# Attention's order written anew: products of one array tiling next to each other, memory products over the whole array, the first pair's loads ahead of the constants

## The chip, the cores and the metric

The kernel runs on one core of a Trainium2 chip. The metric is the device time of one execution in microseconds (us). It is one launch; the host only lays out the inputs. TensorE (PE) does matrix products and transposes, VectorE (DVE), ScalarE (ACT) and GpSimd (POOL) work element by element, and SyncE (SP) issues the DMA transfers between HBM and the on-chip memory. Each engine runs its own instructions strictly in order and waits for the others by semaphores.

## The reference

The reference is a chain of three layers in float32. For 4 batches of 8 heads, with 576 tokens and 64 columns a head:

```python
scores = where(causal, -1e9, q @ k.T / 8); a = softmax(scores); local = a @ v
q_p = phi(q)                      # x + 1 where x > 0, else exp(x)
mem_out = (q_p @ M_prev) / (q_p @ z_prev + 1e-6)
x = sigmoid(beta) * mem_out + (1 - sigmoid(beta)) * local      # 2304 tokens x 512
d = softmax over tokens of x @ phi; slots = d.T @ x            # 32 slots
y = softmax over slots of x @ phi  @  per-expert relu(slots @ w1) @ w2
out = (s * relu(y @ w_in)**2 + b) @ w_out
```

The change lies in the first layer, and in how its work meets what runs beside it.

## The kernel before, in words

Attention goes by pairs of heads: 16 pairs, 4 of a batch. A pair's two heads share a tile, one head in rows 0 to 63 and the other in rows 64 to 127. The work of a pair is cut into small parts, and the list `STEP` (L64) is the order in which one pass of the loop at L611 writes them out: `name:k` means that pass `i` does this part for pair `i + k`. So one pass holds parts of up to five pairs, and since PE, ACT, DVE and POOL keep the written order, `STEP` sets what stands behind what on each engine. SP's transfers are placed by the tile framework when their buffers come free.

The parts, with the engine of each:

- `K`, `R` (SP, L248, L255): loads of a pair's keys, and of its queries, values and memory. `LG` (SP, L559): a piece of `w_in` as 64-bit words; at the last pair it also starts 12 loads of expert weights. `LW` (SP): one buffer of expert weights.
- `S0` to `S4` (PE, L282): scores of 128 queries (64 in `S4`) against all earlier keys, for both heads. For `S0` to `S3` the two heads' products use 64 rows by 128 columns of the array each and run side by side; `S4` uses four quarters of 64 by 64. `Dt.h` (DVE, L296) adds the mask, finds the row's maximum and takes the scores out of PSUM; `Et.h` (ACT) makes the exponential and its sum.
- `Tt.h` (PE, L331): transposes of the probabilities over the whole 128 by 128 array, `t + 1` blocks of 128 columns each (`T4.0` three blocks, `T4.1` two). `Ut.h` takes them out of PSUM, on ACT, for `t = 4` on DVE. `scl` (DVE), `pscl` (POOL) scale the last 64 queries' probabilities ahead of `T4`.
- `V` (PE, L383): probabilities times values, in two column halves of 128 by 64; `O0`, `O1` (ACT) take them out.
- `F0`, `F1`, `F2` (POOL, ACT, DVE): the feature map phi(q). `Z` (POOL, L350): two small copies that put the norm vector behind each head's memory. `M` (PE, L357): the memory products, ten of 65 columns, each on 64 rows by 128 columns. `N` (DVE, L367): the division, into the buffer `mo`.
- `C` (PE): five transposes of the local result. `A`, `A4` (DVE), `P` (POOL, in the last pair DVE): scaling and sum. `X` (PE, L425): transposes of the result, four of 128 by 128 and one of 64 by 64. `Y`, `Y2` (DVE, ACT) take them out; `L` (PE, L439): the routing products, four column quarters of 128 by 32; `B` (DVE).
- `W0`, `Wa` to `Wd` (ACT, POOL, DVE): conversion of a piece of `w_in`. Names in small letters (`dx`, `de`, `dT`, `ds`, `du`, ...) run once a batch.

PSUM has two tiles of two banks for `S` and `M` together, three banks for the transposes, `X`, `C`, `L` and part of `V`, and one for the rest of `V`. A part that takes such a tile waits until the tile taken two (or three) parts earlier has been emptied.

After attention come the merge of the routing sums, the experts (L641 to L712) and the feed-forward layer (L714 to L822). The change does not touch them.

Of the kernel before, what the change touches and what calls it, by code (L numbers as in the profile page):

```python
# [17 lines left out]
B, H, S, D = 4, 8, 576, 64  # L18
NPAIR = B * H // 2
# [16 lines left out]
M_MZ = M_V + 640  # L36
M_END = M_MZ + 130
# [24 lines left out]


STEP = """  # L64
U3.0:1 D2.1:2 E0.0:2 S4:2 U0.1:2 F2:1 D4.0:2 X:0 Z:1 Y:0 T4.1:1 E2.0:2 Y2:0 S3:2 U4.1:1 LG:1 W0:1
D4.1:2 L:0 B:0 dx:0 T2.0:2 E1.0:2 T0.0:2 S0:3 D3.0:2 D0.0:3 V:1 E2.1:2 E4.0:2 fac:1 U2.0:2 D3.1:2
de:0 dT:0 U0.0:2 E3.0:2 dU:0 O0:1 Wa:1 Wb:1 scl:2 O1:1 M:1 Wc:1 D0.1:3 R:4 pscl:2 T1.0:2 gT:0 E1.1:2
ds:0 LW:1 Wd:1 N:1 du:0 K:4 U1.0:2 S1:3 gU:0 T4.0:2 C:1 S2:3 U4.0:2 E3.1:2 F0:2 F1:2 A:1 T1.1:2
E0.1:3 P:1 U1.1:2 T2.1:2 A4:1 U2.1:2 D1.0:3 T3.1:2 D1.1:3 T3.0:2 T0.1:3 U3.1:2 D2.0:3
""".split()  # L70

def strided(ap, *dims):

    return bass.AP(ap.tensor, ap.offset, [list(ap.ap[0])] + [list(d) for d in dims])
# [3 lines left out]
def tile_attention_moe_ffn(  # L78
# [16 lines left out]
    PE, ACT, DVE, POOL, SP = nc.tensor, nc.scalar, nc.vector, nc.gpsimd, nc.sync  # L95
# [6 lines left out]
    ident = cs[:, C_ID:C_ID + 128]  # L102
# [88 lines left out]
    last_pe = [None]  # L191
# [39 lines left out]
    OT, mo, xT = MA[:, 0:640], MA[:, 640:1280].rearrange("p (t d) -> p t d", t=5), MA[:, 0:S]  # L231
# [14 lines left out]
    k_t, qvm_t, x_t, st_t, y_t, o_t, u_t, s_t, t_t, m_t = {}, {}, {}, {}, {}, {}, {}, {}, {}, {}  # L246

    def load_keys(p):  # L248
        if p < NPAIR:
            k_t[p] = KA[:, S * (p % 2):S * (p % 2) + S]  # L250
            for h in range(2):
                r = slice(64 * h, 64 * h + 64)
                SP.dma_start(out=k_t[p][r, :], in_=qk[2 * p + h, r, S:2 * S])

    def load_rest(p):  # L255
        if p < NPAIR:
            qvm_t[p] = QA[p % 3]
            SP.dma_start(out=qvm_t[p], in_=qvm[p])

    def pool_copy(dst, src):  # L260
        POOL.tensor_scalar(out=dst, in0=src, scalar1=1.0, scalar2=0.0, op0=ALU.mult, op1=ALU.add)  # L261
# [14 lines left out]
    def stats(p):  # L276

        if p not in st_t:
            st_t[p] = ap2.tile([128, 28], F32, tag="st", name="st", bufs=5)
        return st_t[p]  # L280
# [66 lines left out]
            evac(strided(PT[p % 2][:, 0, 1344 * i + 512:1344 * i + 513], (64 if i else 448, n), (1984, 2), (1, 64)),  # L347
                 strided(tp[:, 0:1], (128, n), (64, 2), (1, 64)), "v")

    def norm_columns(p):  # L350

        mz = qvm_t[p][:, M_MZ:M_END]
        for h in range(2):
            r = slice(64 * h, 64 * h + 64)
            POOL.tensor_copy(mz[r, 64 + 64 * h:65 + 64 * h], mz[r, 128 + h:129 + h])

    def memory(p):  # L357

        f, mz = FI[p % 2], qvm_t[p][:, M_MZ:M_END]
        y = y_t[p] = pS.tile([128, 1024], F32, tag="s", name="s")  # L360
        for t in range(5):
            for h in range(2):
                r = slice(64 * h, 64 * h + 64)
                PE.matmul(y[:, 512 * h + 65 * t:512 * h + 65 * t + 65], f[r, t * 128:(t + 1) * 128], mz[r, 64 * h:64 * h + 65],  # L364
                          start=True, stop=True)

    def memory_out(p):  # L367
        st, ic, y = stats(p), icst[:, p % 4, :], y_t.pop(p)
        c = slice(8, 18)
        DVE.scalar_tensor_tensor(  # L370
            out=st[:, c].rearrange("p (t h) -> p t h", h=2), in0=strided(y[:, 64:65], (65, 5), (512, 2)), scalar=1e-6,
            in1=ic[:, c].rearrange("p (t h) -> p t h", h=2), op0=ALU.add, op1=ALU.mult)
        DVE.reciprocal(out=st[:, c], in_=st[:, c])
        DVE.tensor_tensor(
            out=mo.rearrange("p t (h d) -> p t h d", h=2), in0=strided(y[:, 0:1], (65, 5), (512, 2), (1, 64)),
            in1=strided(st[:, 8:9], (2, 5), (1, 2), (0, 64)), op=ALU.mult)

    def factors(p):
# [46 lines left out]
    def x_transposes(p):  # L425
        x = x_t[p]
        tp, t2 = t_t[p, "y"] = [pT.tile([128, 512], F32, tag="t", name="t") for _ in range(2)]
        for t in range(4):
            PE.transpose(tp[:, t * 128:(t + 1) * 128], x[:, t, :], ident)  # L429
        last_pe[0] = PE.transpose(t2[:, 0:64], x[0:64, 4, :], ident[0:64, 0:64])  # L430

    def x_out(p, part):
        tp, t2 = t_t[p, "y"]
# [105 lines left out]
    def load_next(place_of=None):  # L539

        n, tag = place_of or next(places, (0, None))
        if n and wnext[0] < len(wkeys):
            load_place(n, tag)
            held.append((wnext[0], n, tag))
# [14 lines left out]
    def load_first(p):  # L559
# [3 lines left out]
    tiles = {"S": scores, "D": maxima, "E": exponentials, "T": transposes, "U": transposed}  # L563
    parts = {
        "K": (load_keys,), "R": (load_rest,), "LW": (lambda p: load_next(),), "LG": (load_first,), "scl": (scale_last,),
        "pscl": (scaled_last,), "F0": (feature, 0), "F1": (feature, 1), "F2": (feature, 2), "Z": (norm_columns,),
        "M": (memory,), "N": (memory_out,), "V": (values,), "O0": (values_out, 0), "O1": (values_out, 1),
        "fac": (factors,), "C": (combine,), "A": (added, 0), "A4": (added, 1), "P": (add_memory,),
        "X": (x_transposes,), "Y": (x_out, 0), "Y2": (x_out, 1), "L": (logits,), "B": (logits_out,),
        "W0": (first_weights, 0), "Wa": (first_weights, 1), "Wb": (first_weights, 2), "Wc": (first_weights, 3), "Wd": (first_weights, 4)}  # L570
    batch = {
# [4 lines left out]
    def part_of(name, p):  # L576
# [11 lines left out]
        if p == NPAIR - 1 and name == "LG":  # L588
            for _ in range(12):
                load_next()  # L590

    SP.dma_start(out=cs, in_=cst)
    SP.dma_start(out=bet, in_=beta)
    SP.dma_start(out=phs, in_=phi)
# [28 lines left out]
    def ps_h():  # L623
        return pH.tile([128, 512], F32, tag="h", name="h")
# [4 lines left out]
    t = ps_h()  # L629
# [57 lines left out]
    for b in range(B):  # L687
# [14 lines left out]
            out=csk[:, :, 1:4:2, :], in0=strided(cex[:, 0, 0:1], (NSLOT, 5), (0, 2), (1, NSLOT)),  # L702
            in1=strided(chi[:, 0, 0:1], (NSLOT, 5), (0, 2), (1, NSLOT)), op=ALU.subtract)
        t = ps_h()
# [3 lines left out]
        t = ps_h()  # L708
# [31 lines left out]
    for _ in range(W_BUFS):  # L740
        t = wp.tile([128, 2 * UNIT], F32R, tag="w", name="w")
# [144 lines left out]
```

## Time and profile before

| what | value |
|---|---|
| median of 3 runs | 555.32 us (553.84 to 561.74) |
| profiled execution | 555.2 us, its span 553.4 us |
| busy share of the span | PE 94%, DVE 66%, ACT 51%, POOL 31% |
| chain that ended last | PE 84%, POOL 7%, DVE 4%, issue 2% |
| attention with its merge | 0 to 250 us of the span |
| experts | 250 to 306 us |
| feed-forward layer | 306 to 553 us |

The chain that ended last is the sequence of work, followed back from the last instruction, in which each step waited for the one before it. PE's busy share counts modelled ends of pipelined products, so a busy PE may still be waiting inside between two products; the start times of successive products tell more. The profiled execution is read against its own time of 555.2 us.

### The profile page before, as it was taken

Reading aid. Unit: us, or ns where it says so; the run is one execution under the profiler, and the core shown is the slowest. Engines: PE = TensorE matmul, PEld = TensorE weight load, DVE = VectorE, ACT = ScalarE, POOL = GpSimd, SP = SyncE. Lnnn points to the kernel's source line nnn. Section 1 sums busy time; section 2 is a strip of 40 time slices with the busy share of each in tenths; the row PEclk is TensorE's granted clock in tenths of the full one; section 3 lists DMA queues with packets and bytes.
Section 4 is the critical chain, followed back from the end, with each engine's and each line's share of the span. In section 5 each row is a group of like instructions: output and inputs, shape, how many; then the busy total and the mean of one; then the engine's idle time right before and its main releaser. Section 6 shows DMA issues by size and latency. Waiting matters only on the chain.

```text
span 553.4 us, 9319 instructions
## 1 busy us (share of the span) xinstructions
PE 520.3 (94%) x3255; PEld 345.3 (62%) x3255; DVE 365.5 (66%) x917; ACT 280.4 (51%) x743; POOL 172.3 (31%) x212
## 2 busy tenths in 40 slices
PE   3999999999999999989999788879999999999997
PEld 1466665666566656653332456558888888888885
DVE  2788887888788878750430999983367465473770
ACT  2877777777777767510221765453542422423322
POOL 0233331332233333300000469996430411404103
PEclk9999999999999999997999999898999999999999
DMA  8799342424242413789995342400020010100101
GB/s 263 249 334 343 126 148 72 150 72 149 69 152 72 149 50 115 245 300 381 368 358 181 126 153 76 152 1 1 1 114 1 10 48 0 59 0 1 57 1 57
DMA packets 26622, 72.01 MB, mean 130 GB/s; under 512 B 3024, under 2 KB 3152, under 8 KB 26576
## 3 DMA queue, kind: packets, MB, share of 16 engines
q1 hardware_dynamic: 26576, 71.42, 37.2%
q8 instruction: 26, 0.43, 0.3%
q14 instruction: 20, 0.16, 0.1%
HBM read 66.69 MB, written 4.72 MB: 129 GB/s over the span
## 4 chain that ended last, share of the span: by engine, by line
PE 84%; POOL 7%; DVE 4%; issue 2%; DMA 1%; ACT 1%; SPq 0%; POOLq 0%; DVEq 0%; ACTq 0%
PE y L799 10%; PE y L801 10%; PE y L800 10%; PE s L290 9%; PE t L335 8%; PE o L394 7%; PE s L364 4%; PE y L662 3%; PE s L294 3%; PE y L646 3%; POOL P L781 3%; PE h L770 3%; POOL R L264 2%; PE t L338 2%; PE t L429 2%
## 5 line engine op out<-in xcount | busy, mean ns | idle before, releaser
L801 PE MATMUL y<-w,R 128*128 128x512 f32 x288 | 114.2, 397 | 6.0 <-POOL R L264 6.0
L799 PE MATMUL y<-w,R 128*128 128x512 f32 x288 | 115.7, 402 | 3.9 <-POOL R L261 3.6
L800 PE MATMUL y<-w,R 128*128 128x512 f32 x288 | 114.1, 396 | 1.4 <-DVE w L759 1.4
L774 ACT ACTIVATE P<-h 128x384 f32<-128x384 f32 x96 | 47.1, 492 | 123.9 <-PE h L770 123.9
L781 POOL TENSOR_SCALAR P<-P,sbt 128x384 f32<-128x384 f32 x31 | 34.7, 1120 | 194.6 <-ACT P L776 194.6
L785 DVE SCALAR_TENSOR_TENSOR P<-P,sbt 128x384 f32<-128x384 f32 x58 | 45.0, 776 | 58.6 <-ACT P L774 58.4
L316 ACT ACTIVATE P<-P,st 128x256 f32<-128x256 f32 (+3 forms) x128 | 71.0, 556 | 5.8 <-DVE st L302 5.8
L801 PEld LDWEIGHTS y<-w,R 128*128 128x128 f32 x288 | 54.6, 190 | 23.3 <-POOL R L264 9.8
L799 PEld LDWEIGHTS y<-w,R 128*128 128x128 f32 x288 | 54.7, 190 | 18.9 <-POOL R L261 6.7
L302 DVE CUSTOM_DVE_ANT_0 P<-s,cs 128x128 f32<-128x128 f32 (+3 forms) x128 | 58.7, 480 | 10.5 <-PE s L290 6.1
L800 PEld LDWEIGHTS y<-w,R 128*128 128x128 f32 x288 | 54.9, 191 | 10.9 <-DVE w L759 1.7
L335 PE MATMUL t<-cs,P 128*128 128x128 f32 x320 | 46.1, 282 | 0.8 <-DVE raw L204 0.6
L290 PE MATMUL s<-R,Q 64*128 64x256 f32 (+3 forms) x176 | 36.8, 499 | 9.5 <-DMA R<-in_qk_dram 8.8
L264 POOL TENSOR_TENSOR R<-P,R 128x384 fp32r<-128x384 f32 x38 | 43.2, 1138 | 3.2
L335 PEld LDWEIGHTS t<-cs,P 128*128 128x128 f32 x320 | 34.2, 141 | 14.4 <-DVE x L417 8.0
L787 DVE SCALAR_TENSOR_TENSOR R<-P,sbt,R 128x384 fp32r<-128x384 f32 x58 | 36.9, 636 | 5.8 <-DVE R L786 0.5
L329 POOL TENSOR_SCALAR P<-P,st 128x576 f32<-128x576 f32 x16 | 16.2, 1014 | 67.1 <-DVE st L325 51.5
L770 PE MATMUL h<-x,R 128*128 128x384 f32 x96 | 34.4, 358 | 0.6 <-ACT P L774 0.6
L202 ACT ACTIVATE raw<-t 128x128 f32<-128x128 f32 (+2 forms) x64 | 25.5, 432 | 15.4 <-PE t L335 15.4
L423 POOL TENSOR_TENSOR x<-x,M 128x512 f32<-128x512 f32 x15 | 19.2, 1280 | 44.4 <-DVE x L417 44.4
L202 ACT ACTIVATE PT<-t 128x128 f32<-128x128 f32 (+2 forms) x64 | 25.2, 433 | 10.4 <-PE t L335 10.4
L786 DVE TENSOR_SCALAR R<-P,sbt 128x384 fp32r<-128x384 f32 x58 | 26.4, 455 | 5.9
(232 smaller groups left out, 868.9 us busy)
## 6 DMA issues: line engine op xcount, KB each, us to landing
w<-in_w_dram SPq DMA_DIRECT2D x18, 512.0 KB, 7.1
raw<-in_w_in_dram SPq DMA_DIRECT2D x8, 1024.0 KB, 5.4
w<-in_w_dram SPq DMA_DIRECT2D x32, 256.0 KB, 5.4
Q<-in_qvm_dram SPq DMA_DIRECT2D x11, 673.0 KB, 5.6
R<-in_qk_dram SPq DMA_DIRECT2D x32, 144.0 KB, 2.8
out_dram<-P SPq DMA_DIRECT2D x18, 256.0 KB, 2.0
raw<-in_w_out_dram SPq DMA_DIRECT2D x4, 1024.0 KB, 4.8
R<-in_qvm_dram SPq DMA_DIRECT2D x5, 673.0 KB, 6.5
```

The lines of the kernel that those rows point to most:

```text
L202: ACT.activation(out=dst, in_=src, func=AF.Copy)
L264: POOL.tensor_tensor(out=dst, in0=a, in1=b, op=ALU.subtract)
L290: PE.matmul(ps[:, 512 * h:512 * h + n], q[r, t * 128:(t + 1) * 128], k[r, 0:n], start=True, stop=True)
L302: DVE.tensor_tensor_reduce(out=Pt[h, t], in0=x, in1=cs[:, C_M2 - n:C_M2], scale=-0.125, scalar=BIG, op0=ALU.add, op1=ALU.min, accum_out=st ...
L316: ACT.activation(out=pt, in_=pt, func=AF.Exp, scale=-1.0, bias=st[:, 18 + c:19 + c], accum_out=st[:, c:c + 1])
L335: PE.transpose(tp[:, kb * 128:(kb + 1) * 128], Pt[i, t][:, kb * 128:(kb + 1) * 128], ident)
L770: PE.matmul(hp[:, 0:TG], G(k * 128, 128), cT[:, g * TG:(g + 1) * TG], start=True, stop=True)
L774: ACT.activation(out=r, in_=hp[:, 0:TG], func=AF.Relu)
L781: POOL.tensor_scalar(out=r, in0=r, scalar1=sbt[:, 0:1], scalar2=sbt[:, 1:2], op0=ALU.mult, op1=ALU.add)
L799: PE.matmul(acc[g, i], hi[:, c], who[k], start=(k == 0), stop=False)
L800: PE.matmul(acc[g, i], hi[:, c], wlo[k], start=False, stop=False)
L801: PE.matmul(acc[g, i], lo[:, c], who[k], start=False, stop=(k == NK - 1))
```

## The change

Four things change.

1. `STEP` is a new list. On PE one pass now runs, in this order: `T4.0:1 T3.1:1 T3.0:1 | S4:2 | T0.0:2 X:0 T1.1:2 | S3:2 S0:3 | L:0 | V:1 | T2.0:2 T1.0:2 dT | S1:3 S2:3 | T2.1:2 gT ds C:1 M:2 T0.1:3 T4.1:2`. Before it ran `S4:2 | X:0 T4.1:1 | S3:2 | L:0 | T2.0:2 T0.0:2 | S0:3 | V:1 | dT M:1 | T1.0:2 gT ds | S1:3 | T4.0:2 C:1 | S2:3 | T1.1:2 T2.1:2 T3.1:2 T3.0:2 T0.1:3`. Bars stand where the tiling of the array changes. `M`, the feature map, `LG` and the conversions of `w_in` come one pass earlier for a given pair; `P`, `LW`, `T3`, `T4.0` and what follows from these come later (`LW` by two passes).
2. `M` becomes five products of 130 columns over the whole array, both heads' memories and norms in one (the zeros of the other head are already in the loaded tile). `Z` goes. `N` reads the new places.
3. `X`'s fifth transpose covers 128 by 128 where it covered 64 by 64.
4. Pair 0's keys and its `qvm` tile (in two transfers, the queries first) are loaded ahead of the four constants.

```diff
 STEP = """
-U3.0:1 D2.1:2 E0.0:2 S4:2 U0.1:2 F2:1 D4.0:2 X:0 Z:1 Y:0 T4.1:1 E2.0:2 Y2:0 S3:2 U4.1:1 LG:1 W0:1
-D4.1:2 L:0 B:0 dx:0 T2.0:2 E1.0:2 T0.0:2 S0:3 D3.0:2 D0.0:3 V:1 E2.1:2 E4.0:2 fac:1 U2.0:2 D3.1:2
-de:0 dT:0 U0.0:2 E3.0:2 dU:0 O0:1 Wa:1 Wb:1 scl:2 O1:1 M:1 Wc:1 D0.1:3 R:4 pscl:2 T1.0:2 gT:0 E1.1:2
-ds:0 LW:1 Wd:1 N:1 du:0 K:4 U1.0:2 S1:3 gU:0 T4.0:2 C:1 S2:3 U4.0:2 E3.1:2 F0:2 F1:2 A:1 T1.1:2
-E0.1:3 P:1 U1.1:2 T2.1:2 A4:1 U2.1:2 D1.0:3 T3.1:2 D1.1:3 T3.0:2 T0.1:3 U3.1:2 D2.0:3
+D2.0:2 T4.0:1 T3.1:1 E0.0:2 U4.1:1 E1.1:2 T3.0:1 D2.1:2 U3.1:1 U4.0:1 S4:2 U3.0:1 T0.0:2 LG:2 P:0
+N:1 D4.0:2 E1.0:2 X:0 D4.1:2 Y:0 U0.0:2 T1.1:2 S3:2 Y2:0 E2.0:2 S0:3 fac:1 L:0 U1.1:2 F2:2 V:1 W0:2
+Wa:2 T2.0:2 B:0 E2.1:2 D3.1:2 R:4 F0:3 LW:-1 E4.0:2 E3.1:2 dx:0 D3.0:2 T1.0:2 D0.0:3 de:0 O0:1 Wb:2
+O1:1 D0.1:3 K:4 dT:0 U2.0:2 S1:3 S2:3 U1.0:2 Wc:2 T2.1:2 dU:0 D1.1:3 E0.1:3 gT:0 D1.0:3 ds:0 gU:0
+scl:2 U2.1:2 Wd:2 du:0 F1:3 pscl:2 C:1 A:1 E3.0:2 M:2 T0.1:3 T4.1:2 A4:1 U0.1:3
 """.split()
...
-            for h in range(2):
-                r = slice(64 * h, 64 * h + 64)
-                PE.matmul(y[:, 512 * h + 65 * t:512 * h + 65 * t + 65], f[r, t * 128:(t + 1) * 128], mz[r, 64 * h:64 * h + 65],
-                          start=True, stop=True)
+            PE.matmul(y[:, 191 * t:191 * t + 130], f[:, t * 128:(t + 1) * 128], mz, start=True, stop=True)
...
-        last_pe[0] = PE.transpose(t2[:, 0:64], x[0:64, 4, :], ident[0:64, 0:64])
+        last_pe[0] = PE.transpose(t2[:, 0:128], x[:, 4, :], ident)
...
+            for c in (slice(0, S), slice(S, M_END)) if p == 0 else (slice(0, M_END),):
+                SP.dma_start(out=qvm_t[p][:, c], in_=qvm[p, :, c])
...
+    load_keys(0)
+    load_rest(0)
     SP.dma_start(out=cs, in_=cst)
```

## Rows read from the trace of the kernel before

**Rows 1.** Windows: length, busy PE, PEld, DVE, ACT, POOL; clock, DMA share, GB/s.

```profile
121.22:134.68 13.46, 13.46 (x114) 8.43 (x113) 11.38 (x39) 10.10 (x32) 4.22 (x6) 1.00 0.45 152
250.00:306.00 56.00, 53.33 (x343) 17.20 (x343) 13.64 (x46) 11.41 (x28) 0.00 (x0) 0.95 0.89 324
```

**Rows 2.** Timeline of PE in one pass: start, us to the last end, engine, line.

```profile
121.22 0.49 PE L290 MATMUL s<-R,Q 64*128 64x128 f32 x4
...
124.50 1.33 PE L364 MATMUL s<-Q,R 64*128 64x65 f32 x20
125.76 0.44 PE L335 MATMUL t<-cs,P 128*128 128x128 f32 x2
126.13 0.70 PE L290 MATMUL s<-R,Q 64*128 64x256 f32 x4
126.77 0.55 PE L338 MATMUL t<-cs,P 128*128 128x128 f32 x3
...
127.79 0.92 PE L290 MATMUL s<-R,Q 64*128 64x384 f32 x4
128.64 1.75 PE L335 MATMUL t<-cs,P 128*128 128x128 f32 x14
130.31 1.19 PE L294 MATMUL s<-R,Q 64*64 64x288 f32 x8
131.43 0.66 PE L429 MATMUL t<-cs,x 128*128 128x128 f32 x4
...
132.59 1.13 PE L290 MATMUL s<-R,Q 64*128 64x512 f32 x4
133.65 0.42 PE L442 MATMUL t<-M,phs 128*32 128x128 f32 x8
...
134.68 0.49 PE L290 MATMUL s<-R,Q 64*128 64x128 f32 x4
```

**Rows 3.** Timeline of PE behind the last pair's values.

```profile
233.56 0.88 PE L196 MATMUL s<-cs 128*128 128x64 f32 x6
234.37 1.33 PE L364 MATMUL s<-Q,R 64*128 64x65 f32 x20
235.63 0.66 PE L406 MATMUL t<-cs,M 128*128 128x128 f32 x4
```

**Rows 4.** Groups by line and shape: busy us, mean ns of one, idle before.

```profile
L189 DVE SCALAR_TENSOR_TENSOR win<-raw,win 128x512 int32<-128x512 int32 x16 | 16.2, 1010 | 0.1
...
L417 DVE TENSOR_TENSOR x<-t,st 128x512 f32<-128x512 f32 x16 | 10.9, 681 | 0.0
...
L415 DVE TENSOR_TENSOR x<-t,M 128x128 f32<-128x128 f32 x16 | 4.5, 281 | 0.0
...
L204 DVE COPY PT<-t 128x256 f32<-128x256 f32 x8 | 3.3, 416 | 0.0
...
L324 DVE TENSOR_SCALAR st<-st,eb 128x1 f32<-128x1 f32 x16 | 3.3, 207 | 0.0
```

**Rows 5.** Timeline of DVE, the first pair's maxima.

```profile
9.81 0.29 DVE L302 CUSTOM_DVE_ANT_0 P<-s,cs 128x128 f32<-128x128 f32 x1 [4.31 <-PE s L290]
...
10.66 0.42 DVE L302 CUSTOM_DVE_ANT_0 P<-s,cs 128x256 f32<-128x256 f32 x1 [0.34 <-PE s L290]
11.01 0.08 DVE L302 DVE_READ_ACCUMULATOR2_ANT st<- 128x1 f32 x1
...
12.07 0.56 DVE L302 CUSTOM_DVE_ANT_0 P<-s,cs 128x384 f32<-128x384 f32 x1 [0.63 <-PE s L290]
```

**Rows 6.** Page, DMA issues: count, KB each, median us to landing.

```profile
Q<-in_qvm_dram SPq DMA_DIRECT2D x11, 673.0 KB, 5.6
R<-in_qk_dram SPq DMA_DIRECT2D x32, 144.0 KB, 2.8
...
cs<-in_cst_dram SPq DMA_DIRECT2D x1, 528.0 KB, 3.4
```

**Rows 7.** Timeline of DVE, the last pair's scaling.

```profile
236.95 0.68 DVE L417 TENSOR_TENSOR x<-t,st 128x512 f32<-128x512 f32 x1
```

More of the change, by code (lines that the diff above doesn't have):

```diff
@@ L248, in load_keys @@
     def load_keys(p):
-        if p < NPAIR:
+        if p not in k_t:
             k_t[p] = KA[:, S * (p % 2):S * (p % 2) + S]
@@ L255, in load_rest @@
     def load_rest(p):
-        if p < NPAIR:
+        if p not in qvm_t:
             qvm_t[p] = QA[p % 3]
-            SP.dma_start(out=qvm_t[p], in_=qvm[p])
+            for c in (slice(0, S), slice(S, M_END)) if p == 0 else (slice(0, M_END),):
+                SP.dma_start(out=qvm_t[p][:, c], in_=qvm[p, :, c])
     def pool_copy(dst, src):
@@ L348, in transposed @@
                  strided(tp[:, 0:1], (128, n), (64, 2), (1, 64)), "v")
-    def norm_columns(p):
-        mz = qvm_t[p][:, M_MZ:M_END]
-        for h in range(2):
-            r = slice(64 * h, 64 * h + 64)
-            POOL.tensor_copy(mz[r, 64 + 64 * h:65 + 64 * h], mz[r, 128 + h:129 + h])
     def memory(p):
@@ L361, in memory @@
         for t in range(5):
-            for h in range(2):
-                r = slice(64 * h, 64 * h + 64)
-                PE.matmul(y[:, 512 * h + 65 * t:512 * h + 65 * t + 65], f[r, t * 128:(t + 1) * 128], mz[r, 64 * h:64 * h + 65],
-                          start=True, stop=True)
+            PE.matmul(y[:, 191 * t:191 * t + 130], f[:, t * 128:(t + 1) * 128], mz, start=True, stop=True)
     def memory_out(p):
@@ L370, in memory_out @@
         DVE.scalar_tensor_tensor(
-            out=st[:, c].rearrange("p (t h) -> p t h", h=2), in0=strided(y[:, 64:65], (65, 5), (512, 2)), scalar=1e-6,
+            out=st[:, c].rearrange("p (t h) -> p t h", h=2), in0=strided(y[:, 128:129], (191, 5), (1, 2)), scalar=1e-6,
             in1=ic[:, c].rearrange("p (t h) -> p t h", h=2), op0=ALU.add, op1=ALU.mult)
@@ L374, in memory_out @@
         DVE.tensor_tensor(
-            out=mo.rearrange("p t (h d) -> p t h d", h=2), in0=strided(y[:, 0:1], (65, 5), (512, 2), (1, 64)),
+            out=mo.rearrange("p t (h d) -> p t h d", h=2), in0=strided(y[:, 0:1], (191, 5), (64, 2), (1, 64)),
             in1=strided(st[:, 8:9], (2, 5), (1, 2), (0, 64)), op=ALU.mult)
@@ L565, in tile_attention_moe_ffn @@
         "K": (load_keys,), "R": (load_rest,), "LW": (lambda p: load_next(),), "LG": (load_first,), "scl": (scale_last,),
-        "pscl": (scaled_last,), "F0": (feature, 0), "F1": (feature, 1), "F2": (feature, 2), "Z": (norm_columns,),
+        "pscl": (scaled_last,), "F0": (feature, 0), "F1": (feature, 1), "F2": (feature, 2),
         "M": (memory,), "N": (memory_out,), "V": (values,), "O0": (values_out, 0), "O1": (values_out, 1),
```

## The prediction

> **What bounds the kernel now.** I read the page's chain first: most of it is PE. Then the windows: in a steady attention pass of 13.46 us PE is busy for all of it at full clock (1.00), while DVE has 11.38 us of work, ACT 10.10 and POOL 4.22 [rows 1]. So a pass ends when PE's own list ends, and the question is what PE spends its list on. The timeline of PE answers that, read by start times, since the durations overlap [rows 2].
>
> The score groups start 0.64 us (S1, 126.13 to 126.77), 0.85 (S2) and 1.06 (S3, 132.59 to 133.65) ahead of the group behind them: 0.21 for each further 128 columns, and 0.21 left over that no column explains. Two transposes behind other work take 0.37 (125.76 to 126.13), fourteen take 1.67 (128.64 to 130.31): 0.108 a block and 0.15 left over. The group T4.0 with C behind it (126.77 to 127.79, eight blocks) takes 1.02, which is 8 x 0.108 + 0.15: two different parts with the same tiling pay the rest once. So PE pays about 0.15 us (0.21 where scores stand alone) each time the array's tiling changes, part in running dry, part in loading the first weights with nothing beside it. The other groups, less their columns at the same rate: S4 1.12 - 0.97 = 0.15; S0 and V together (121.22 to 124.50) 3.28 - 0.21 - 2.67 = 0.40; M 1.26, of which ten steps of 0.112 are products, 0.14 left; X with T4.1 behind it (131.43 to 132.59) 1.16 - 7 x 0.108 = 0.40, for three groups, as X's fifth block has a tiling of its own; L about 0.12.
>
> **The change, part by part.** *Fewer changes of tiling.* The old pass has 15 groups: S0 to S3 at 0.21, six of transposes at 0.15, X's fifth block 0.09, S4 0.15, V 0.19, M 0.14, L 0.12, 2.4 us in all. The new one has eight: S4 0.15, three of the whole array at 0.15, S3 with S0 and S1 with S2 at 0.21 each, L 0.12, V 0.19, sum 1.33. PE alone saves 1.1 us, and its pass is 12.35. No trace shows two score groups in a row: bounds for the two seams 0 and 0.21 each; I take 0, as T4.0 with C paid nothing.
>
> *M over the whole array.* Ten steps as before, now 130 columns at 0.21 per two steps of 128, so 0.108 each, against weight loads that already set 0.112. Six plain whole-array products of 64 columns take 0.81 to the next group [rows 3], less 0.15 for the change 0.11 each: the same step. So M keeps 1.12. Between transposes and plain products of one tiling no row shows the seam: bounds 0 and 0.15 for each of two; I take 0.05 together, near the seam that cost nothing.
>
> *Waits.* The new pass has a tight ring. S4 needs the PSUM tile of S2, which D2.1 empties, and DVE's list from S1 on reads D1.1, D1.0, scl, Wd, A, A4, D2.0, U4.1, D2.1. Durations: 2 x 0.42 and 2 x 0.55 [rows 5], about 0.2 and 0.2 for scl's two, 1.01, 0.68, 0.28, 0.42 [rows 4], together 4.7; one starts some 0.08 before the last ends (10.66 to 11.01 for 0.42, [rows 5]), so 4.0 to 4.7. From S1's result to S4, PE has S2 0.74, 22 blocks x 0.108, M 1.12 and 0.15 for the change, less 0.2 us until the result is out: 4.2. PE therefore waits 0 to 0.5 us a pass; I take 0.15, between them. T4.0, T4.1 and T3.0 need PSUM that A, A4 and U4.1 empty in the same stretch, the same wait and not a second one. L needs Y, which now stands behind N on DVE: Y's end and L's turn fall within 0.1 us of each other. A pass is then 12.55, 0.9 less. DVE with 11.4 of 12.55 still has 1.1 us of idle time, ahead of D1.1, where it takes up what is late in the first half.
>
> *Moves that cost nothing while that holds.* The feature map, the conversions of w_in and M go one pass earlier, with the same instructions. LG's 1 MB is issued once Wd has freed its buffer, 5 us ahead of W0, and W0's result isn't wanted for 2 us more. P goes behind A, at the pass's start on POOL, 1.3 us that N's last step and X wait for: A ends 1.5 us before S4, X starts 1.3 after. T4 waits for pscl (1 us on POOL behind scl), with about 0.3 to spare. Z was 0.4 us of idle POOL. R waits for V now, 3 us ahead of need as before. LW's twelve loads go two passes later, on an SP queue with DMA at 0.45 [rows 1]; the last four, and the first tagged places, are issued at the last pair's LG, a pass before they were. The 64-row transposes made 128-row cost the step they had, 0.108.
>
> *Start.* The first maximum runs at 9.81, behind scores that waited for the keys [rows 5]. Ahead of them went constants (528 KB) and qvm (673 KB), then keys of 2 x 144 KB [rows 6]. Now 0.58 MB of about 1.5 MB are enough for S0, but the mask still comes last of the same bytes. So S0 goes 3 to 4 us earlier, the maximum by 8.2 to 8.5 us, 1.4 earlier. With W0 of pair 0 a pass earlier, behind 1 MB, some of ACT's time may be lost again; bounds 0 and 3.5, I take 1.5, near the mask's arrival.
>
> *End.* Between the last pair's V and C stood M, 1.26 us from 234.37 to 235.63 [rows 3], and the division ahead of A (236.95, [rows 7]), which C's result could have fed at about 236.2. Both are now done a pass before. C then follows V's evacuation: 1.3 earlier, and A 0.7 more. I take 2.0; 0 if C's evacuation binds elsewhere, 4 if the gaps ahead of it close too.
>
> **Sum.** 16 pairs, of which the first and last passes are ramps: 14 x 0.9 = 12.6, plus 1.5, plus 2.0, is 16.1. From the profiled 555.2 us (span 553.4; the median of the runs shown is 555.3, so it stands for them) that gives 539. Experts and feed-forward move as a block. In 250 to 306 PE is busy for 53.3 of 56 us with DMA at 0.89 [rows 1], so weights are close to binding there; their buffers come free relative to attention's end, and w_in's and the feature map's a pass earlier, so I add nothing.
>
> **Rivals.** *DVE's ring closes late.* If the ring takes its 4.7 us and one seam costs something, a pass is 13.1 or so: 0.6 more in 14 passes, 547. For it: DVE would be busy for 90% of such a pass, with every wait in order. Against it: its idle time sits ahead of D1.1. Chance 0.17.
>
> *The order saves nothing.* If PE's left-over time goes with each new tile, not with the tiling, only start and end gain: 552. T4.0 with C speaks against it. Chance 0.06.
>
> *The memory products double.* If a product of 130 columns over the whole array can't overlap its weights, M takes 20 steps' time: 1.12 more a pass, 15.7 in all, 555, no change. The six plain products speak against it, with 64 columns only [rows 3]. The Trainium skill (TensorEngine Tiling (Array Packing), Overview) promises up to twice the speed for a contraction of 64 rows cut into two row tiles, which is what the change gives up; by that, M alone would cost this much more. Here weight loads, not columns, set the old step, so no such gain stood in the trace. Chance 0.05.
>
> *The clock falls: slower.* The new pass runs transposes and M together for some 3.7 us (T2.1 to T3.0), where the longest run was 1.67. If PE fell to half its clock in that stretch, it would take 3.7 more in each pass, 51 in 14: 590. It passes the old time from the fifth pass on that falls (16.1 / 3.7). For it: the clock is below 1 around the experts [rows 1]. Against it: 1.00 with fourteen transposes in a row, and M parts the new run. The Trainium skill (TensorE: Matmul & The Clock Gate, Part 4: PE-mode transpose) says that transposes don't count as busy time for the clock in the way products do, which speaks for it; no row here bears it out. Chance 0.05.
>
> **How the numbers follow.** My forecast, PE bound at about 12.5 us a pass, has 0.67: 539, of itself 533 (seams and ring 0: 15.4, start 2.5, end 4) to 544 (the ring's wait at 0.4: 9.1, start and end 1 each). Before and after can be told apart from no change by about 2%, 11 us. The range takes in the ring's case and ends short of the doubled product: 533 to 551, some 8 in 10. Faster by over 2% means under 544: nearly all of 0.67 and a little of the ring's, 0.68. Within 2%: the ring, the order that saves nothing, the doubled product, 0.27. Slower by over 2%: the clock, 0.05.
>
> **What would show it.** Successive S4 starts on PE 12.4 to 12.7 apart in passes without a batch's end, S0 0.22 to 0.23 long behind S3, and steps of 0.11 in M. Waits of PE's S4 or T3.0 for DVE (D2, U4) of 0.1 to 0.2 each would be the ring; over 0.5 make the ring's case. S0 of the first pair near 5 us, its first maximum near 8.4. C of the last pair less than 1 us behind V. The stretch of the experts as long as before, 56 us. The forecast is wrong if the clock's row falls under 1.0 in a pass, if W0 waits for its transfer by more than 2 us, or if the weights arrive late behind a shorter end of attention.

## The result, and the profile after

The changed kernel takes **536.34 us** (median of 4 runs, 534.34 to 538.49) against 558.53 (median of 4, 553.84 to 562.1) in the same comparison: the ratio is 0.9608, 95% interval 0.9505 to 0.9712. It is faster, and the time is 2.7 us under the forecast of 539.0. Run again later in five rounds it gave 538.18 us, ratio 0.9645 (0.9589 to 0.9701). In all comparisons of this study the kernel before took 552.36 to 556.13 us at a mean granted clock of 0.986 to 0.994 and 559.46 to 562.31 us at one of 0.972 to 0.977, so the median of a few of its runs moves with how many of each there are. The profiled executions differ by less than the medians of this comparison: span 553.39 before, 532.55 after (534.34 us with what lies around it), at mean clocks of 0.987 and 0.990. Those 20.8 us are what is taken apart here.

Windows of the kernel after, columns as in [rows 1]: a pass of attention from one S4 to the next, the experts' first layer, and a stretch at half clock.

```profile
163.26:175.70 12.44, 12.44 (x104) 8.52 (x103) 10.79 (x39) 10.21 (x32) 3.57 (x4) 1.00 0.41 143
233.40:248.40 15.00, 15.00 (x133) 4.91 (x136) 0.62 (x1) 1.67 (x3) 0.00 (x0) 1.00 1.04 388
...
289.50:296.30 6.80, 6.49 (x17) 2.96 (x10) 4.85 (x8) 2.33 (x4) 2.79 (x3) 0.50 0.43 154
```

The pass of 13.46 us [rows 1] is now 12.44 (12.44 or 12.45 in each pass without a batch's end, from the third on), still with PE busy for all of it and at full clock. PE of that pass, the rows that answer to [rows 2]; what counts is again the distance from one start to the next.

```profile
163.26 1.19 PE L295 MATMUL s<-R,Q 64*64 64x288 f32 x8
164.37 0.33 PE L336 MATMUL t<-cs,P 128*128 128x128 f32 x1
...
165.44 1.35 PE L291 MATMUL s<-R,Q 64*128 64x512 f32 x8
166.72 0.43 PE L433 MATMUL t<-M,phs 128*32 128x128 f32 x8
...
167.33 2.76 PE L385 MATMUL o<-raw,R 128*64 128x512 f32 x20
...
170.72 1.35 PE L291 MATMUL s<-R,Q 64*128 64x256 f32 x8
171.99 0.55 PE L336 MATMUL t<-cs,P 128*128 128x128 f32 x3
...
172.81 0.27 PE L398 MATMUL t<-cs,M 128*128 128x128 f32 x1
172.92 1.28 PE L356 MATMUL s<-Q,F 128*128 128x130 f32 x10
174.04 0.27 PE L336 MATMUL t<-cs,P 128*128 128x128 f32 x1
...
175.70 0.70 PE L295 MATMUL s<-R,Q 64*64 64x288 f32 x3
```

There are eight groups. S3 with S0 takes 1.28 (165.44 to 166.72): the 1.06 of S3 alone and one step of 0.21 for S0's 128 columns, so the seam between two score groups is nothing. M takes 1.12 from its first product to the next transpose (172.92 to 174.04), and 0.11 separates C's last block from it, the step of a block: no seam on either side.

The end of attention, PE from the last pair's values on (it answers to [rows 3]):

```profile
216.59 2.76 PE L385 MATMUL o<-raw,Q 128*64 128x512 f32 x20
219.28 0.88 PE L196 MATMUL s<-cs 128*128 128x64 f32 x6
220.11 0.66 PE L397 MATMUL t<-cs,M 128*128 128x128 f32 x4
```

The products that keep PE warm run behind the values now and C follows them; M is gone from here. DVE of the same stretch, the scaling of [rows 7]:

```profile
220.80 0.69 DVE L408 TENSOR_TENSOR x<-t,st 128x512 f32<-128x512 f32 x1 [3.86 <-PE t L397]
```

And the start, which answers to [rows 5] and [rows 6]: PE's first scores, DVE's first maximum, then ACT's first piece of w_in (W0), each with what it waited for.

```profile
5.24 1.65 PE L291 MATMUL s<-R,Q 64*128 64x128 f32 x8 [5.24 <-DMA Q<-in_qvm_dram]
...
8.84 0.29 DVE L303 CUSTOM_DVE_ANT_0 P<-s,cs 128x128 f32<-128x128 f32 x1 [8.84 <-DMA cs<-in_cst_dram]
...
15.09 0.69 ACT L181 ACTIVATE win<-raw 128x512 f32<-128x512 f32 x1 [0.26 <-DMA raw<-in_w_in_dram]
```

From the second pair's S2 on PE runs without a gap to the first pair's values. First the kernel before, then after:

```profile
18.75 0.92 PE L290 MATMUL s<-R,Q 64*128 64x384 f32 x4
...
24.99 2.32 PE L394 MATMUL o<-PT,Q 128*64 128x512 f32 x12
```

```profile
17.64 0.92 PE L291 MATMUL s<-R,Q 64*128 64x384 f32 x4 [0.53 <-DVE st L303]
...
18.94 1.38 PE L356 MATMUL s<-Q,F 128*128 128x130 f32 x10
20.16 0.27 PE L336 MATMUL t<-cs,P 128*128 128x128 f32 x1
...
25.14 2.05 PE L385 MATMUL o<-PT,Q 128*64 128x512 f32 x10
```

S2 stands 1.11 us earlier than before, and the values 0.15 later: M of the first pair, 1.22 from 18.94 to 20.16, now comes ahead of them. From S2 to the values it is 6.24 before and 7.50 after; of the runs below, the one in the old order has the same 6.24, and six in the new one 7.49 or 7.50.

**Where the 20.8 us came from**, by the start of the same PE groups in both profiles:

| stretch | before | after | gain |
|---|---|---|---|
| start to pair 0's first values | 24.99 | 25.14 | -0.15 |
| 14 passes, to pair 14's values | 195.91 | 181.94 | 13.97 |
| to the products of the selection (L624) | 27.35 | 24.82 | 2.53 |
| these, to the experts' first layer | 2.19 | 1.50 | 0.69 |
| experts' first layer | 17.38 | 15.01 | 2.37 |
| to the feed-forward's first product | 38.82 | 38.82 | 0.00 |
| feed-forward to PE's last product | 242.31 | 241.28 | 1.03 |
| behind it | 4.44 | 4.04 | 0.40 |

The starts on which the attention rows rest, before (L394, L631) and after (L385, L624); the others stand above:

```profile
220.90 2.79 PE L394 MATMUL o<-PT,R 128*64 128x512 f32 x20
...
230.87 2.76 PE L394 MATMUL o<-raw,Q 128*64 128x512 f32 x20
...
248.25 1.74 PE L631 MATMUL h<-sel,uacc 128*128 128x32 f32 x8 [1.23 <-DVE sel L520]
```

```profile
207.08 2.76 PE L385 MATMUL o<-PT,R 128*64 128x512 f32 x20
...
231.90 1.05 PE L624 MATMUL h<-sel,uacc 128*128 128x32 f32 x8 [1.22 <-DVE sel L511]
```

The -0.15 of the first row is less than what one start differs from another: with the start of the changed kernel the first values came at 25.14, 25.25 and 26.30 in three profiles, with that of before at 24.99 and 26.34 in two. Attention itself gave 16.35 us. The 3.06 about the experts' first layer is the clock, not the order. Two windows of the kernel before show it, the first in that layer's beginning and the second behind it:

```profile
250.44:255.20 4.76, 4.76 (x24) 1.19 (x28) 0.00 (x0) 0.00 (x0) 0.00 (x0) 0.50 1.01 373
...
255.20:267.82 12.62, 12.62 (x113) 4.00 (x108) 0.64 (x1) 1.67 (x3) 0.00 (x0) 1.00 1.05 389
```

The granted clock was 0.50 (the lower of the two levels) for 6.8 us from 248.4 on, through the last small products of the selection and the first 4.8 us of the layer: 24 products took the time of some 42 at full clock (113 in 12.62 us in the second row). Half of the 4.76 us is 2.38, the table's 2.37, and the products of the selection, 1.74 long there, take 1.05 after, which is the 0.69. After, this stretch fell at 289.5, in the feed-forward. The feed-forward's 1.03 lies inside the 240.6 to 242.7 us that it took in the runs below, whose feed-forward is the same code, so it is no finding.

### The profile page after: what moved, and what is told of

The parts are those of the page before. It is cut to its first block, busy times and chain, and to the rows that moved or that the text cites. A ratio compares the mean times of both kernels' runs of the same rounds, so it can differ in the third digit from the quotient of the medians.

```text
span 532.6 us, 8936 instructions
## 1 busy us (share of the span) xinstructions
PE 503.5 (95%) x3095; PEld 345.7 (65%) x3095; DVE 356.0 (67%) x917; ACT 281.1 (53%) x743; POOL 162.6 (31%) x180
## 4 chain that ended last, share of the span: by engine, by line
PE 84%; POOL 7%; DVE 4%; ACT 2%; issue 1%; DMA 1%; SPq 0%; POOLq 0%; ACTq 0%; DVEq 0%
PE y L792 11%; PE y L794 11%; PE y L793 11%; PE t L336 8%; PE o L385 8%; PE s L291 8%; PE y L655 4%; PE s L295 4%; PE s L356 3%; PE y L639 3%; POOL P L774 3%; PE h L763 3%; POOL R L265 3%; PE t L339 2%; PE y L660 2%; POOL R L262 1%
## 5 line engine op out<-in xcount | busy, mean ns | idle before, releaser
L317 ACT ACTIVATE P<-P,st 128x128 f32<-128x128 f32 (+3 forms) x128 | 71.2, 557 | 0.4
L336 PE MATMUL t<-cs,P 128*128 128x128 f32 x320 | 54.2, 285 | 0.0
L265 POOL TENSOR_TENSOR R<-P,R 128x384 fp32r<-128x384 f32 x38 | 44.7, 1177 | 3.2
L291 PE MATMUL s<-R,Q 64*128 64x128 f32 (+3 forms) x176 | 32.5, 476 | 8.9 <-DMA Q<-in_qvm_dram 5.2
L330 POOL TENSOR_SCALAR P<-P,st 128x576 f32<-128x576 f32 x16 | 16.1, 1007 | 66.7 <-DVE st L326 52.5
L183 POOL TENSOR_SCALAR win<-win 128x512 f32<-128x512 f32 x16 | 10.3, 644 | 76.3 <-ACT win L181 76.3
L202 ACT ACTIVATE PT<-t 128x256 f32<-128x256 f32 (+2 forms) x64 | 25.9, 432 | 14.0 <-PE t L336 13.9
L779 DVE TENSOR_SCALAR R<-P,sbt 128x384 fp32r<-128x384 f32 x58 | 27.5, 474 | 6.0
L202 ACT ACTIVATE raw<-t 128x256 f32<-128x256 f32 (+2 forms) x64 | 25.8, 433 | 6.6 <-PE t L336 6.5
```

Source lines behind the costliest of these rows:

```text
L202: ACT.activation(out=dst, in_=src, func=AF.Copy)
L265: POOL.tensor_tensor(out=dst, in0=a, in1=b, op=ALU.subtract)
L291: PE.matmul(ps[:, 512 * h:512 * h + n], q[r, t * 128:(t + 1) * 128], k[r, 0:n], start=True, stop=True)
L317: ACT.activation(out=pt, in_=pt, func=AF.Exp, scale=-1.0, bias=st[:, 18 + c:19 + c], accum_out=st[:, c:c + 1])
L336: PE.transpose(tp[:, kb * 128:(kb + 1) * 128], Pt[i, t][:, kb * 128:(kb + 1) * 128], ident)
```

## The experiments

Unless it says otherwise, a kernel is the changed one with the edit that is shown. A pass is the distance between two starts of S4 on PE.

**One seam more.** T1.1, two transposes, is put between S3 and S0.

```
- ... U0.0:2 T1.1:2 S3:2 Y2:0 E2.0:2 S0:3 ...
+ ... U0.0:2 S3:2 T1.1:2 Y2:0 E2.0:2 S0:3 ...
```

> The changed kernel with one PE part moved: T1.1 goes from ahead of S3 to between S3 and S0. Same instructions, same tiles; two more groups of one tiling in each pass. Theory 1 (each change of tiling costs PE 0.15 us, 0.21 at scores): a pass of 12.45 becomes 12.81, some 5 us over 14 passes. Theory 2 (the gain came from fewer instructions, ten memory products where there were twenty and no norm copies): the pass stays 12.45. Theory 3 (the old order lost its time in waits for DVE and ACT that the new one takes away): the pass stays within 0.05 of 12.45, as nothing that PE waits for is moved.

542.23 us, beside 555.25 for the kernel before. The pass is 12.76, 0.31 longer, with two more changes of tiling. PE of this kernel at the seam:

```profile
169.01 1.13 PE L291 MATMUL s<-R,Q 64*128 64x512 f32 x4
170.07 0.44 PE L336 MATMUL t<-cs,P 128*128 128x128 f32 x2
170.44 0.49 PE L291 MATMUL s<-R,Q 64*128 64x128 f32 x4
170.86 0.42 PE L433 MATMUL t<-M,phs 128*32 128x128 f32 x8
```

S3, the transposes and S0 take 1.06, 0.37 and 0.42: 0.37 is two blocks at 0.108 and 0.15, and S0 is back from 0.21 to its 0.42 of before. Theory 1 holds, 0.05 under its number; theories 2 and 3 had 12.45.

**Two seams.** The same, and T1.0 between S1 and S2.

```
- D3.0:2 T1.0:2 D0.0:3 ... S1:3 S2:3 ...
+ D3.0:2 D0.0:3 ... S1:3 T1.0:2 S2:3 ...
```

> As the run with T1.1 between S3 and S0, and T1.0 also between S1 and S2: four more groups of one tiling than the changed kernel. Theory 1: 12.45 + 2 x 0.36 = 13.17, some 10 us in all, half of the whole gain back without an instruction more. Theories 2 and 3: 12.45 to 12.5.

546.63 us; the pass is 13.11, 0.66 longer than the changed kernel's. Its window, and the two score groups with T1.0 between:

```profile
172.38:185.49 13.11, 13.11 (x105) 8.33 (x104) 10.90 (x39) 10.33 (x32) 3.53 (x4) 1.00 0.37 126
```

```profile
166.82 0.70 PE L291 MATMUL s<-R,Q 64*128 64x256 f32 x4
167.45 0.44 PE L336 MATMUL t<-cs,P 128*128 128x128 f32 x2
167.82 0.92 PE L291 MATMUL s<-R,Q 64*128 64x384 f32 x4
```

None, one and two seams make 12.45, 12.76 and 13.11: the price is paid for each, PE busy throughout, and neither DVE (10.90) nor a wait takes it up.

**M in halves of the rows.** The changed order, but with M as it was before: two row tiles, and POOL's copy of the norm's column.

```
-            PE.matmul(y[:, 191 * t:191 * t + 130], f[:, t * 128:(t + 1) * 128], mz, ...)
+            for h in range(2):
+                r = slice(64 * h, 64 * h + 64)
+                PE.matmul(y[:, 512 * h + 65 * t:512 * h + 65 * t + 65], f[r, t * 128:(t + 1) * 128], mz[r, 64 * h:64 * h + 65], ...)
```

> The changed kernel with the memory products in two row halves again (twenty of 65 columns' records, norm copies on POOL back), all else as changed. Theory 1: the products' own steps stay 0.112, and M becomes a group of its own that also cuts the run of transposes in two: 0.29 more, a pass of 12.74, 4 us in all. Theory 2: ten records more a pass, 1.1 us: 13.5. If the doubling that the skill's array packing speaks of were lost by the change, M here would take 0.56 less and the pass fall to 12.2.

541.91 us, the pass 12.74. PE around M, 0.20 and 1.27 from C's last block to M and through M where the changed kernel has 0.11 and 1.12:

```profile
176.53 0.27 PE L408 MATMUL t<-cs,M 128*128 128x128 f32 x1
176.73 1.33 PE L365 MATMUL s<-Q,F 64*128 64x65 f32 x20
178.00 0.33 PE L336 MATMUL t<-cs,P 128*128 128x128 f32 x1
178.16 0.71 PE L339 MATMUL t<-cs,P 128*128 128x128 f32 x5
```

With the 0.16 from T's first block to the next, where the changed kernel has 0.11, that is 0.09, 0.15 and 0.05: 0.29, two changes of tiling. With one of them in the 1.27, the products themselves take the same in halves.

**M over the whole array, alone.** The order of before, with M over the whole array; without the copy that it needed.

```
-            for h in range(2): ... f[r, ...], mz[r, 64 * h:64 * h + 65]
+            PE.matmul(y[:, 191 * t:191 * t + 130], f[:, t * 128:(t + 1) * 128], mz, ...)
```

> The kernel before with the memory products over the whole array alone (no norm copies), its order kept. M then stands behind V and ahead of T1.0, with which it shares the tiling. Theory 1: one change of tiling fewer, 13.46 to 13.31, 2 us in all. Theory 2: ten instructions fewer, 12.4. Theory 3: 13.46.

The pass is 13.36, 0.10 under the 13.46 of before and 0.05 above theory 1, which counts one change of tiling less, as M stands ahead of T1.0 and now shares its tiling. M itself gains next to nothing, what it gives is that it may stand among the transposes. The total was 560.40 beside 555.25, which the order can't explain: the clock fell to half for 20.5 us.

```profile
240.70:261.20 20.50, 19.03 (x86) 10.09 (x89) 4.04 (x16) 1.62 (x8) 0.00 (x0) 0.50 0.79 288
```

**Constants first.** The changed kernel with the first pair's loads behind the constants again, issued by its own first step.

```
-    load_keys(0)
-    load_rest(0)
     SP.dma_start(out=cs, in_=cst)
...
```

> The changed kernel with the four constants loaded ahead of the first pair again (keys and the two pieces of qvm behind them, as the loop issues them). Theory 1 (the first maximum sets the start, and it waits for the mask, which the change moved behind more bytes while it moved the scores ahead): the first maximum goes from 9.0 to about 9.8, and the first values and all behind them come 0.5 to 1 us later. Theory 2 (my sum: the loads are worth 1.5): 1.5 later. Theory 3 (what follows in the first passes waits for the 1 MB of w_in, not for the mask): within 0.3 of the changed kernel.

The first maximum came at 10.01 in place of 8.84, but W0 at 15.23 in place of 15.09 and the first values at 25.26 in place of 25.14. From W0 on to the last pair's values (216.70 against 216.59) everything is 0.1 later: theory 3, the 1.2 at the first maximum is lost again within 6 us. The 0.1 itself is no finding, as the same start alone differs by 1.2 us from run to run; neither 1.5 us nor 0.5 to 1 is to be seen for the loads' order, though one run each can't exclude the smaller. The total of 540.78 (beside 552.36) has 13.7 us of half clock from 227.7 on in it.

**The mask earlier.** The constants between the first pair's queries and the rest of its loads.

```
             for c in (slice(0, S), slice(S, M_END)) if p == 0 else (slice(0, M_END),):
+                if p == 0 and c.start:
+                    SP.dma_start(out=cs, in_=cst)
                 SP.dma_start(out=qvm_t[p][:, c], in_=qvm[p, :, c])
...
-    SP.dma_start(out=cs, in_=cst)
```

> The changed kernel with the constants' tile (mask and identity, 528 KB) loaded behind the first pair's keys and queries and ahead of the rest of its qvm tile (378 KB). Theory 1: the first maximum comes 1.2 to 1.5 us earlier than 9.0, the attention's end about 1 us earlier. Theory 3: the first maximum earlier, but the first values within 0.3 of the changed kernel's 25.1.

534.60 us. The first maximum at 8.28, 0.56 earlier (1.2 to 1.5 before 9.0 was theory 1), and the first values at 25.44, 0.30 later, which lies inside the 25.14 to 26.30 of the changed kernel's own start. No gain came through; what the mask gave, ACT lost again at W0, which waited for its transfer:

```profile
15.42 0.67 ACT L181 ACTIVATE win<-raw 128x512 f32<-128x512 f32 x1 [0.82 <-DMA raw<-in_w_in_dram]
```

**The first piece split.** The same, and the first megabyte of w_in in two transfers.

```
-            load_float64(("wi", p // 4, p // 2 % 2))
+            load_float64(("wi", p // 4, p // 2 % 2), apart=p == 0)
```

> As the run with the mask earlier, and the first 1 MB of w_in loaded in two transfers of 512 KB, so that pair 0's conversion waits for the first alone. In three runs so far the first values started 10.02 to 10.05 us behind the start of this conversion on ACT, whatever came earlier. Theory 3 (this transfer sets the start): no wait for it, the conversion at 14.3 to 14.8 in place of 15.42, the first values 10.0 behind it, at 24.3 to 24.9. Theory 1 (the mask sets it): first values stay at 25.1 to 25.4.

W0 no longer waits, and the first values come at 23.80, 1.34 earlier than in the changed kernel's profile and outside the spread of its start (25.14 to 26.30). The run of both together, with the same start, has them at 24.17.

```profile
13.75 0.68 ACT L181 ACTIVATE win<-raw 128x512 f32<-128x512 f32 x1
```

From W0 to these values it is 10.05 us, as in the changed kernel (25.14 - 15.09), 10.02 to 10.07 in four more runs with its order and 10.47 in the run of both together. Of the first megabyte's transfer the trace says that it landed 8.5 us behind its issue in the changed kernel, the two halves 6.1 us (median) here. The maximum came at 7.55, 0.73 before that of the last run, so not all of the 1.34 is the transfer's.

The total was 537.19, with the gain at the last pair's values (215.24 against 216.59) and 0.9 left of it at the experts' first layer: a stretch of half clock.

**Wide warm products.** The products that only keep PE busy have 512 columns in place of 64, and fewer stand in each place.

```
-    wt=[3, 4, 4, 4, 3, 3],
+    wt=[1, 1, 1, 1, 1, 1],
-            PE.matmul(scratch[:, 0:64], ident, ident[:, 0:64], start=True, stop=True)
+            PE.matmul(scratch[:, 0:512], ident, cs[:, 0:512], start=True, stop=True)
```

> The changed kernel with the products that keep PE busy in the merge made 512 columns wide in place of 64, one where there were 3 or 4. Theory 1 (what the end-to-end gain has beyond the 17 us at the experts' start, and the spread of its runs, is the granted clock in merge, experts and the feed-forward's first part): no stretch at half clock between 216 and 283 us, runs near 534 and none near 538. Theory 2 (stretches at half clock come whatever PE does there): spread as before, 534 to 539.

536.91 us in five rounds, ratio 0.9634 (0.9577 to 0.9692), from 535.26 to 539.0: the spread of theory 2, where theory 1 had none near 538. Its profile has full clock from 226 to 311, but so has the changed kernel's up to 289.5.

**Both together.** The split first piece, the mask earlier, the wide warm products.

> Mask earlier, first piece split and wide warm products together. If both hold, 0.5 to 0.8 us under the wide-warm run: 533 to 534, 0.955 to 0.965 of the kernel before. If the start doesn't move, the same as the wide-warm run.

536.65 us, ratio 0.9614 (0.9548 to 0.9680), 0.26 under the wide warm run where 0.5 to 0.8 was expected. The half-clock stretch stood where the warm products were to keep it away:

```profile
226.00:232.20 6.20, 4.88 (x25) 2.18 (x25) 2.67 (x10) 0.93 (x6) 0.00 (x0) 1.00 0.77 263
232.20:239.00 6.80, 6.35 (x34) 2.28 (x37) 0.29 (x1) 0.00 (x0) 0.00 (x0) 0.50 1.01 364
```

Theory 2: wide products don't hold the clock.

**The changed kernel again**, beside the two before on the same chip.

> The changed kernel itself again, beside the others: 534 to 539 by the clock in its second half, 0.955 to 0.97 of the kernel before; its attention passes 12.45 us and its experts' start at 233 to 234 in every case.

538.18 us, ratio 0.9645 (0.9589 to 0.9701). Its passes are 12.45, but its experts' first layer starts at 234.34, behind the 233 to 234 expected: 6.9 us of half clock begin at 231.9. The three intervals overlap, so none of the three can be told from the others, and no version here is shown to beat the change.

**Seven groups.** The mask earlier, the split first piece, and X moved ahead of S4 into the long whole-array run, with T0.0 and T1.1 joined to T2.0 and T1.0: nothing stands between S4 and S3.

```
- ... T3.0:1 D2.1:2 U3.1:1 U4.0:1 S4:2 U3.0:1 T0.0:2 LG:2 P:0
- N:1 D4.0:2 E1.0:2 X:0 D4.1:2 Y:0 U0.0:2 T1.1:2 S3:2 ...
+ ... T3.0:1 U4.0:1 D2.1:2 U3.1:1 LG:2 P:0 X:0 S4:2 U3.0:1
+ N:1 D4.0:2 E1.0:2 D4.1:2 Y:0 S3:2 ...
+ ... D3.0:2 Wb:2 Wc:2 de:0 T0.0:2 T1.1:2 O0:1 U0.0:2 O1:1 T2.0:2 U1.1:2 T1.0:2 D0.0:3 ...
```

> The changed kernel with the mask ahead of the first pair's other loads and the first weights of the experts' input product in two transfers (as in the run of the first piece split), and with a pass of seven groups of one tiling in place of eight: X stands ahead of S4 in the long whole-array run, and the short transposes T0.0 and T1.1 stand with T2.0 and T1.0. Theory 1 (each change of tiling costs PE 0.15 us and PE's list sets the pass): PE's list 12.35 - 0.15 = 12.20, a pass 12.3 with the two delays of 0.04, 13 passes x 0.15 = 2.0 us earlier at the experts' start than the first piece split: experts' first layer at 230.5, total about 535 where a stretch of half clock falls as in the changed kernel. Theory 2 (the ring of waits closes: X now wants P and U4.0 earlier, S4 wants D2.1 behind them): S4 or X waits on PE by 0.15 or more a pass, pass 12.45 or longer, nothing gained. Theory 3 (DVE, with some 11.4 us of work, sets the pass): pass 12.4 or more with PE waiting for DVE ahead of several groups.

547.41 us, ratio 0.9855 (0.9821 to 0.9890): most of the gain is gone. The pass is 12.94, where PE's list alone would be 12.20. Of one pass from S4 on PE (with L of the next pass), the weight loads of the scores, and DVE:

```profile
170.99 1.19 PE L297 MATMUL s<-R,Q 64*64 64x288 f32 x8
172.11 1.74 PE L293 MATMUL s<-R,Q 64*128 64x512 f32 x8
174.01 0.43 PE L435 MATMUL t<-M,phs 128*32 128x128 f32 x8 [0.16 <-DVE st L373]
...
186.94 0.43 PE L435 MATMUL t<-M,phs 128*32 128x128 f32 x8 [0.15 <-DVE M L204]
```

```profile
173.33 0.33 PEld L293 LDWEIGHTS s<-R,Q 64*128 64x128 f32 x4 [0.92 <-PE s L293]
```

```profile
172.73 0.52 DVE L311 CUSTOM_DVE_ANT_0 P<-s,cs,st 128x288 f32<-128x288 f32 x1
...
173.17 0.69 DVE L204 COPY M<-t 128x512 f32<-128x512 f32 x1
```

S3 and S0 take 1.90 in place of 1.28. Scores share two PSUM tiles: S0 takes the one that S4 left, and S4's maxima end at 173.25 (172.73 + 0.52), and S0's weights come at 173.33. Their row names S3's products as what they waited for; that they were held for the maxima is read from the two times. Then L waits for Y, the copy that starts at 173.17 behind these maxima and ends at 173.86; the row of the next pass names it (M L204). S0 starts 1.25 behind S3 (0.96 in the changed kernel) and L 0.65 behind S0 (0.32). So theory 2 names the kind of cause, a ring of waits, but not the place: it closed at S0 and L, not at X or S4. In the changed order the 1.07 us of X, T0.0 and T1.1 between S4 and S3 is what these maxima run under.

## Why the prediction was right, step by step

**Fewer changes of tiling: right.** 14 passes gave 13.97, 1.0 each, for 0.9 forecast. The price of 0.15 per change, read from starts in [rows 2], came back in both directions: fewer groups in the change, and one, two and a pair of seams put in again at 0.31, 0.66 and 0.29 a pass. With that the rival that the order saves nothing falls. **The seams** taken at 0 (scores behind scores) and 0.05 (M among transposes) are both 0.

**M over the whole array: right.** 1.12 forecast and measured; the rival of a doubled product falls. The Trainium skill (TensorEngine Tiling (Array Packing), Overview) promises up to twice the speed from cutting such a contraction into row tiles; the run of M in halves shows none of it for this product: the pass is 0.29 longer with the halves, two changes of tiling, and the products themselves take the same.

**The ring's wait: mis-sized.** 0.15 was taken, and a pass is 0.09 over PE's list of 12.35. It lies in two runs of transposes, 1.07 (164.37 to 165.44) where eight blocks make 1.01, and 3.71 (171.99 to 175.70) where 22 blocks and M make 3.65. PE's rows show no wait for DVE in a steady pass, so no row shows it to be the ring's. The ring that closes late, the rival at 13.1 us a pass, did not come either (DVE's share of such a pass would be 11.4 of 13.1, 87%, not 90%). The bound of 0.5 was not idle, though: the run of seven groups shows a ring of this kind closing for 0.74 a pass (12.94 less 12.20) once 1.07 us of cover is moved away. The prediction had looked at S4, T3.0 and L, where it left 0.1 us, but not at S0.

**Start: the step that failed.** 1.5 us were forecast and -0.15 came, and beside the spread of one start (1.2 us and more) no gain is to be seen. The loads did most of what was expected: S0 at 5.24 for 5, but the first maximum at 8.84 for 8.2 to 8.5, 0.97 earlier than before where 1.4 was forecast. What failed is "moves that cost nothing": M goes one pass earlier, and the sum booked its 1.26 as a gain at the end without charging the first pass, where M's 1.22 now stands ahead of the first values on a PE with no gap left. The 7.50 from S2 to these values, in place of 6.24, came back in seven profiles of this order, with M whole or in halves, and the old order kept its 6.24 with M whole too; no run moves M alone, so its place as the cause is read from these rows. W0, moved too, adds its part: on ACT it stood at 22.94 before, behind the second pair's S2, and stands ahead of that at 15.09 now, and it waits 0.26 for a transfer issued at 6.61 that took 8.5 us. Where the mask came 0.56 earlier, W0 waited 0.82, and only where its transfer was split did the values of this order come earlier, by 1.0 to 1.3. The sign named for it, a wait of more than 2 us, was too high. Constants first shows the same from the other side: a first maximum 1.17 later left the values within the spread, 0.12 later.

**End: right, if the start pays for M.** C follows the values by 3.52 in place of 4.76 (1.24, forecast 1.3). A stands 4.21 behind the last values in place of 6.08 (220.80 - 216.59; 236.95 - 230.87), 1.87 earlier for the 2.0 of the sum. The 2.53 of the table is 0.46 ahead of the last values, these 1.24, 0.55 from C to X and 0.28 behind X. Of 3.5 for start and end together 2.38 came, short by about one M; the passes gave 1.4 more than forecast, so the sum of 16.1 stands beside 16.35 measured up to the selection's products. That the two misses, 1.1 too much and 1.4 too little, nearly cancel is luck.

**What the sum left out.** "Experts and feed-forward move as a block" held for the order and not for the clock: 3.06 us of the profile's gain are half-clock products that fell in the experts' first layer before and not after. This is an accident of the two executions shown: the same layer takes 15.0 where no such stretch falls in it and 16.6 to 17.9 where one does, and one fell there in the changed kernel's own second profile (17.2). The sum was near for the change; a part of the distance to the median is this.

**The clock's rival falls.** The granted clock is 1.00 through the run of transposes and M from 171.99 to 175.70, which is 3.71 us as forecast, in all passes. The rule that transposes don't count for the clock (the Trainium skill, TensorE: Matmul & The Clock Gate, Part 4: PE-mode transpose) is not borne out by a run with M's ten steps among 22 blocks; no run here has such a stretch without them.

**Open.** What starts a stretch of half clock near the end of attention. Every run of the study that lost its clock there had PE partly idle before (4.88 of 6.20 us in the window above), but so had the runs that kept it; wide warm products neither prevented it nor can be shown to help. How much of the medians' difference of 21 to 22 us is the clock, the runs of the later five rounds say: the kernel before at a mean clock of 0.986 or more (five runs of eleven) has a median of 554.26, 16.1 above the changed kernel's 538.18 (six runs, all at 0.987 or more), and with all eleven it is 21.3. So about 5 us of it go with the kernel before's runs at the lower clock. The profile shown of the changed kernel, 534.34, is the fastest of its ten runs, so its 20.8 is too much as well. Why that kernel had such runs there, and the changed one none in ten, was not tried.

## What to carry to other kernels

Where PE's list is the pass, read its timeline by starts, subtract columns at one rate, and count the changes of tiling: here each cost 0.15 us, and putting products of one tiling side by side gave back nearly all of them. Before moving a short group away, ask what runs under it: S4's maxima and the copy Y behind them on DVE needed the 1.07 us of other work between S4 and S3, and moving it away to save one change of tiling, 0.15, made the pass 0.5 longer. A step that goes one pass earlier is gained at the end only as far as the first pass has room for it: charge it there, with the transfer that it waits for.

## What the runs showed that was not expected

The clock of PE fell to its lower level for 3.4, 6.8, 13.7 or 20.5 us about attention's end, in other places and lengths in runs of the same kernel, and a total moved by up to 6 us with it (the constants-first run: marks 0.1 later than the changed kernel's up to the last values, the experts' second layer 5.5 later). Distances between marks inside attention came back to 0.01 us in nearly all passes of all runs of one order, so they separate 0.1 us; the time of a mark itself carries the start's spread of 1.2 us, and by totals even five rounds did not separate 1 us.

PE's first products are slow although the row of the granted clock says 1.00 there, and for how long differs from run to run. In the changed kernel PE starts at 5.24, waits for the mask from about 6.9 to 9.40, and S4 of the first pair takes 1.93 us (11.39 to 13.32); with the constants first, PE starts at 8.58, has no gap, and the same S4 takes 1.13 (12.56 to 13.69). The gap is not the whole cause, though: without one, S4 takes 1.36 in the kernel before (12.36 to 13.72) and 2.11 in the run of M alone (12.70 to 14.81), where PE starts at 8.77 and 8.79. This is a part of the start's spread, and why it differs is open.
